# Fifty-one products of zeros placed among the early work of TensorE in an attention and MLP kernel

## The chip, the cores and the metric

The kernel runs on one core of one Trainium2 chip, as one launch. Time is device microseconds of that core. Each kernel was timed several times; the median is compared. One further execution of each was recorded by the hardware profiler, and its rows are those shown here. PE is TensorE, DVE is VectorE, ACT is ScalarE, POOL is GpSimd and SP is SyncE, which issues the DMAs.

## The reference

```python
# q, k, v: 4 batches x 8 heads x 1152 x 64
q_pool = q.reshape(B, H, S // 2, 2, D).mean(axis=3)          # 576 pooled queries per head
scores = q_pool @ k.transpose(0, 1, 3, 2) / np.sqrt(D)
scores = scores - np.max(scores, axis=-1, keepdims=True)
attn = np.exp(scores)
attn = attn / (np.sum(attn, axis=-1, keepdims=True) + 1e-09)
x = (attn @ v).transpose(0, 2, 1, 3).reshape(2304, 512)
h = x @ w_in                                                 # 512 x 2048
out = np.maximum(0.01 * h, h) @ w_out                        # 2048 x 512
```

## The kernel before

Attention goes over 32 heads (hd 0 to 31). For a head, K, Q and V are loaded (load_k, load_q, load_v); POOL adds the pairs of queries (q_sum, line 459); PE transposes K (k_tr, line 409, five transposes) and Q (q_tr, line 467, three) against an identity; ACT and DVE split the results into a high and a low part (k_hi, k_lo, q_hi, q_lo; lines 296, 425, 476 to 482). PE then forms score tiles of 128 queries by 384 keys (qk, line 515), fourteen steps in a head, and DVE reduces each to its maximum (vmax, line 518). The maxima are negated, transposed by PE (m_tr, line 529), copied (m_cp, line 533) and brought by a DMA (m_dma, line 536) into a row of the low part of Q. The second score product, transposed (qkt, lines 548 and 549, four products of 288 columns a tile), can then be exponentiated by ACT as it is (exp, line 553). POOL sums (esum, line 558), and PE multiplies by V (pv, line 566) and forms the row sums (r_mm, line 577). Weights are loaded and split meanwhile, and the MLP (l1, line 709; l2 and l2s, lines 790 to 824) follows block by block, partly among the attention.

The order on each engine is not written by hand. Every piece of work is a step with a priority (lower goes first), a cost on its engine in estimated us, dependencies, and the buffers that it takes. A scheduler (class Scheduler) simulates the engines with these costs while the program is built: it looks for the earliest time at which any pending step could start, and among the steps that can start by then takes the one with the lowest priority. A table of shifts (SHIFT) is added to the priorities by name and head. What the scheduler picks is emitted at once, so its order is the order of instructions on each engine. `deps` have to end first, `order` steps only have to have started, and `takes` names a buffer and the steps after which it is free again.

PSUM has eight banks; bank 5 is the tag "o", which pv takes for each head from its first half on, and the tag "xb" is the buffer in SBUF for a block of x, taken by x_load after the heads of the first batch. Banks 4 and 7, and for a time 6, are the tag "t" for transposes and score tiles. Ahead of the scheduler's steps the program makes the identity on POOL and clears five tiles on DVE (lines 1042 to 1046).

Of the kernel before, what the change touches and what calls it, by code (L numbers as in the profile page):

```python
# [19 lines left out]
RT = 0.5  # L20
AHEAD = 14
MT = 5
START = 200
MAXES = 4
PVP = 2.5
# [86 lines left out]
MLP = ("x_load", "x_hi", "x_lo", "ws_load", "l1", "post", "l2", "o_evac", "o_out")  # L112


def shift(name, n, *more):

    ends = PHASES["weights" if name in WEIGHTS else "mlp" if name in MLP else "attention"]
    part = {"w_f32": 0, "post": 1}.get(name)
    by = SHIFT.get(name if part is None else name + str(more[part]), ())
    phase = sum(n >= x for x in ends)  # L120
    return by[phase] if phase < len(by) else 0
# [132 lines left out]
def tile_pooled_attention_moe(  # L254
# [15 lines left out]
    nc = tc.nc  # L270
# [19 lines left out]
    ENG = {"ACT": nc.scalar, "DVE": nc.vector, "POOL": nc.gpsimd}  # L290

    def f32(t):
        return t.bitcast(F32)
# [43 lines left out]
    def new(tag, slot, dtype=None):  # L337
        own, i = slot[0]
        if own == "bank":
            return banks[:, i, :] if len(slot) == 1 else banks[:, i:i + len(slot), :]  # L340
        shape, dt = (shapes[tag], F32R) if tag in shapes else spec[tag][1:3]
        dt, shape = dtype or dt, list(shape)
        if own == tag:
            return sb.tile(shape, dt, tag=f"{own}{i}", name=own)
        n = 1
        for x in shape[1:]:
            n *= x
        t = sb.tile(FIXED[own] if own in FIXED else spec[own][1], dt, tag=f"{own}{i}", name=own)
        if len(t.shape) > 2:
            old = "abc"[:len(t.shape) - 1]  # L350
            t = t.rearrange(f"p {' '.join(old)} -> p ({' '.join(old)})")
        t = t[:shape[0], :n]
        names = "abcd"[:len(shape) - 1]
        return t.rearrange(f"p ({' '.join(names)}) -> p {' '.join(names)}", **dict(zip(names, shape[1:])))
# [130 lines left out]
        )  # L485

    qz = {}

    def q_side(hd, e, i):
        qz[hd] = 128 * i[0][1]  # L490
        nc.scalar.copy(out=qzs[:, qz[hd] + 64:qz[hd] + 128], in_=f32(qh[hd])[:, SP - 64:])
# [354 lines left out]
    def trs(*rows):  # L846
        return {"PE": sum(0.01 + 0.00077 * r for r in rows)}

    def act(n, psum=False):
        return (0.16 if psum else 0.19) + n / 1200.0  # L850

    def dve(n, rate=1, psum=False):
        return (0.15 if psum else 0.13) + n / 960.0 / rate
# [7 lines left out]
    def step(fn, *a, prio, eng, lat=0.0, deps=(), order=(), takes=(), lock=False):  # L861
        prio += shift(fn.__name__, *a)
        sch.add((fn.__name__, *a), partial(fn, *a), prio, eng, lat, [d for d in deps if d], [d for d in order if d], takes, lock)

    def sp(n, nbytes, run=512):
        return dict(eng={"SP": 0.5 * n}, lat=nbytes / 300e3 * max(1.0, 512 / run))

    for hd in range(NHD):
        p0 = 5.0 * hd
        pr = p0 - AHEAD - (0 if hd else START)  # L870
        prev = hd - 1 if hd else None

        def after(*key):
            return [(key[0], hd - 1, *key[1:])] if hd else []
# [4 lines left out]
        for g in range(2):  # L879
            hold = [(f, hd, x) for f in ("k_hi", "k_lo") for x in ((2,) if g else (0, 1))]  # L880
            step(k_tr, hd, g, prio=pr + 0.1 * g, eng=trs(*[128] * (1 if g else KT // 2)),
                 deps=[("load_k", hd)] + ([("k_tr", hd, 0)] if g else after("k_tr", 1)),
                 takes=[("t", hold, TR)] + ([] if g else [("ka", [last, ("k_dup", hd)])]))
            for x in (2,) if g else (0, 1):
                n = 128 if g else 512
# [6 lines left out]
        if 0 < hd < len(qls):  # L892
# [3 lines left out]
             takes=[("t", hold, TR), ("qh", [last]), ("ql", [last])])  # L896
        for x in range(2):
            for y in range(2):
# [3 lines left out]
             takes=[("qz", [("qk", hd, NQ - 1, 1)])])  # L902
        pm = p0 - MAXES - (0 if hd else START)
        ready = [("q_hi", hd, x, y) for x in range(2) for y in range(2)]
        todo = [(i, 0) for i in range(NQ)] + [(NQ - 1, 1)] + [(i, c) for c in (1, 2) for i in range(NQ - 1)]
        for n, (i, c) in enumerate(todo):
# [4 lines left out]
                 takes=[("t", [("vmax", hd, i, c)])] + ([] if n else [("st", [("m_tr", hd)])]))  # L911
            step(vmax, hd, i, c, prio=pm - 1 + 0.02 * n, eng={"DVE": dve(w, psum=True)}, deps=[("qk", hd, i, c)])
        step(m_side, hd, prio=pm - 2, eng={"ACT": act(2)}, deps=[("vmax", hd, NQ - 1, x) for x in range(2)])
        step(vneg, hd, prio=pm - 2, eng={"DVE": 0.17}, deps=[("m_side", hd)] + [("vmax", hd, *x) for x in todo])
        step(m_tr, hd, prio=pm - MT, eng=trs(128), deps=[("vneg", hd)], takes=[("t", [("m_cp", hd)])])
        step(m_cp, hd, prio=pm - 2, eng={"ACT": act(128, True)}, deps=[("m_tr", hd)], takes=[("ms", [("m_dma", hd)])])
        step(m_dma, hd, prio=pm - 2, **sp(1, 0.01e6), deps=[("m_cp", hd)], order=[("q_lo", hd, x) for x in range(2)])
        ready += [("k_lo", hd, x) for x in range(3)] + [("k_dup", hd), ("m_dma", hd)] + [("q_lo", hd, x) for x in range(2)]
        done = ("pv", hd, NBU - 1)
        ns = KT - 1 - direct(hd)  # L920
        for t in range(KT):
# [4 lines left out]
                 takes=[("e", [("pv", hd, b), ("esum", hd, max(t, 1)) if t <= ns else ("r_mm", hd)])])  # L926
            if 0 < t <= ns:
                step(esum, hd, t, prio=p0 - 4 + 0.5 * t, eng=pool(2 * HW, "esum" if hd < 14 else "late"), lock=True, deps=[("exp", hd, t), ("exp", hd, 0) if t == 1 else ("esum", hd, t - 1)],
                     takes=[("sm", [("r_mm", hd)])] if t == 1 else [])
        for b, (t0, t1) in enumerate(BURSTS):  # L930
            step(pv, hd, b, prio=p0 + 0.5 * t1 + PVP, eng=mm4(*[HW] * (t1 - t0)),
                 deps=[("exp", hd, t) for t in range(t0, t1)] + [("load_v", hd), ("pv", hd, b - 1) if b else ("pv", hd - 1, NBU - 1) if hd else None],
                 takes=[] if b else [("o", [("norm", hd)])])
        step(r_mm, hd, prio=p0 + 4.5 + RT, eng=mm4(*[HW] * ((2 + direct(hd)) // 2)), deps=[("esum", hd, ns)] + [("exp", hd, t) for t in range(ns + 1, KT)],
             takes=[("t", [("r_cp", hd)])])
# [13 lines left out]
    for n, i in enumerate(seq):  # L949
        o = i // NF  # L950
# [11 lines left out]
    for p in range(FH):  # L962
# [5 lines left out]
        for n in range(4):  # L968
            deps = [("w_sum", p, n % 2)] + ([("w_sum", p, 1)] + [("l2", FAST - 1, 0, 1, x) for x in (p,)] if n == 0 else [])
            takes = [("w2" if p == 0 and n == 1 else "w1", last)] if n and not (p == 0 and n == 2) else []  # L970
# [3 lines left out]
    for i in range(NBLK):  # L974
# [5 lines left out]
        order = [x * FH + p for p in range(FH) for x in (1, 0)] if fast else list(range(NF))  # L980
        for at, f in enumerate(order):
# [4 lines left out]
                 order=[("ws_load", i if at else i - 1, was) if at or i else None], takes=[("ws", [("l1", i, f, 2)], 0 if i else 1)])  # L986
            for part in range(3):
                dep = [("l1", i, f, part - 1) if part else prev, ("w_lo", 2 * NF - 1) if i == 1 and f == 0 else None]
                dep += [("ws_load", i, f), ("x_hi", i)] if part == 0 else [("x_lo", i)] if part == 1 else []
                takes, begun = [], []  # L990
                if part == 0 and at % 2 == 0:
                    if fast:
                        n = (i - FAST) * FH + fp - DEEP
                        begun = [("l2s", FAST + n // FH, n % FH, 0 if n % FH == FH - 1 else None)] if n >= 0 else []
                        takes = [("ml", [("g_act", i, fp)])]
                    else:
                        takes = [("ml", [("post", i, fp, 0)]), ("gg", [("l2", i, hf, 1, f + 1)], 0 if i else 1)]
# [11 lines left out]
        for p in range(FH if fast else 0):  # L1009
            banks_of = [[("o_mix", i, n) for n in x] for x in ((1,), (3,), (5, 7), (6,))]  # L1010
            for b in range(4) if p == FH - 1 else (None,):
                last = ("l2s", i, p, b - 1) if b else ("l2s", i, p - 1, None) if p else ("l2s", i - 1, FH - 1, 3) if i > FAST else ("l2", i - 1, 1, 1, NF - 1)
                n = 21 if b is None else 3 if b == 3 else 6
                step(l2s, i, p, b, prio=pr + p + LAG, eng=mm(*[256] * n), deps=[last, ("g_lo", i, p)] + [("w_rest", p, x) for x in range(4)],
                     takes=[("ml", x) for x in banks_of] if p == 0 else [])
        if fast:
            need = (0, 0, 1, 1, 2, 2, 3, 2)
            order_of = ((), (0,), (0, 1), (2,), (2,), (4,), (3, 4), (6,))
            for n in range(8):
                eng = {"DVE": dve(256, psum=True)} if n else {"ACT": act(256, True), "DVE": dve(256, psum=True)}  # L1020
                step(o_mix, i, n, prio=-50, eng=eng, deps=[("l2s", i, FH - 1, need[n])] + [("o_mix", i, x) for x in order_of[n]],
                     takes=[] if n else [("raw", [("o_mix_out", i, j)], 1) for j in range(2)])
# [3 lines left out]
        for hf in range(2):  # L1026
            for j in range(2):
                fs = range(hf * FH, hf * FH + FH)
                last = ("l2", i, hf, 0, fs[-1]) if j else ("l2", i, 0, 1, FH - 1) if hf else ("l2", i - 1, 1, 1, NF - 1) if i else None
                for f in fs:  # L1030
                    step(l2, i, hf, j, f, prio=pr + 15, eng=mm(512, 512, 512),
                         deps=[("l2", i, hf, j, f - 1)] if f != fs[0] else [last, ("w_lo", NF + fs[-1])] + [("post", i, x, 2) for x in range(hf * FP, hf * FP + FP)],
                         takes=[("ml", [("o_evac", i, hf, j)])] if f == fs[0] else [])
                step(o_evac, i, hf, j, prio=-50, eng={"DVE": dve(512, psum=True)} if hf else {"ACT": act(512, True), "DVE": dve(512, psum=True) + 0.3},
                     deps=[("l2", i, hf, j, fs[-1])] + ([("o_evac", i, 0, j)] if hf else []), takes=[] if hf else [("raw", [("o_out", i, j)], 1)])
# [42 lines left out]
```

## Time and profile before

| | us |
|---|---|
| median of 3 runs | 911.78 |
| lowest and highest | 909.09, 915.53 |
| the profiled execution | 910.16 |
| its span, first to last instruction | 908.4 |
| PE busy | 872.6 |
| DVE busy | 538.0 |
| ACT busy | 459.4 |
| POOL busy | 453.9 |

The profiled execution's time is compared with the medians, its span with the rows of the trace; 1.8 us lie around the span. Times in rows are us from the span's start.

### The profile page before, as it was taken

To read this page: it belongs to the slowest core of one execution; us is meant where nothing else is said; L and a number is where in the kernel's file an instruction comes from. 1 tells how busy PE (TensorE), PEld (TensorE's weight loads), DVE (VectorE), ACT (ScalarE), POOL (GpSimd) and SP (SyncE) were. 2 spreads that over 40 slices of the span, in tenths; PEclk is the share of its full clock that TensorE was granted. 3 is DMA by queue.
4 is the path that set the end of the run, shared out by engine and by line. 5 is a ranking of instruction groups with operands and counts; after the bars stand their busy time and mean duration, and the time that the engine had idled before them with its cause. 6 is when DMAs were issued, how large, how long until landed. Compare 5 with 4: busy or idle time off the path is not lost.

```text
span 908.4 us, 17330 instructions
## 1 busy us (share of the span) xinstructions
PE 872.6 (96%) x6408; PEld 731.9 (81%) x6408; DVE 538.0 (59%) x1140; ACT 459.4 (51%) x905; POOL 453.9 (50%) x352
## 2 busy tenths in 40 slices
PE   5898899999999999999999999999999999999997
PEld 3676666678877778887887888787898999999997
DVE  6788878777665655555455554601179863645343
ACT  3676786865656575545566555444143422323231
POOL 2457677686778676766676766766321010110000
PEclk9999999999999999999999999999999999999999
DMA  5588785865745854445367434434664767776660
GB/s 157 143 229 258 200 252 165 239 184 160 251 112 170 238 171 134 121 128 153 85 148 183 117 112 110 134 97 130 222 196 178 236 226 221 230 220 216 201 229 30
DMA packets 113269, 158.74 MB, mean 175 GB/s; under 512 B 21632, under 2 KB 80160, under 8 KB 113184
## 3 DMA queue, kind: packets, MB, share of 16 engines
q1 hardware_dynamic: 113184, 157.64, 59.2%
q8 instruction: 50, 0.82, 0.4%
q14 instruction: 35, 0.29, 0.1%
HBM read 130.02 MB, written 17.90 MB: 163 GB/s over the span
## 4 chain that ended last, share of the span: by engine, by line
PE 76%; DMA 12%; DVE 4%; ACT 3%; SPq 2%; issue 1%; POOL 0%; DVEq 0%; ACTq 0%; POOLq 0%
PE banks L709 21%; PE banks L566 11%; PE banks L790 11%; PE banks L515 7%; PE banks L548 7%; PE banks L549 6%; PE banks L822 3%; PE banks L824 3%; PE banks L823 3%; DMA rt<-rs 2%; DMA raw<-in_moe_w_out_dram 2%; DMA raw<-in_moe_w_in_dram 2%; PE banks L409 2%; PE banks L577 2%; DMA qn<-in_q_dram 1%
## 5 line engine op out<-in xcount | busy, mean ns | idle before, releaser
L553 ACT ACTIVATE e<-banks 128x576 f32<-128x576 f32 x288 | 185.4, 650 | 158.4 <-PE banks L549 156.1
L558 POOL TENSOR_TENSOR sm<-sm,e 128x576 f32<-128x576 f32 x168 | 242.8, 1446 | 44.0 <-ACT e L553 37.3
L518 DVE TENSOR_REDUCE stat<-banks 128x1 f32<-128x384 f32 (+1 forms) x448 | 218.9, 535 | 69.5 <-PE banks L515 64.5
L548 PE MATMUL banks<-qh,ka 128*128 128x288 f32 x576 | 171.2, 313 | 5.5 <-ACT e L553 5.3
L549 PE MATMUL banks<-ql,kb 128*128 128x288 f32 x576 | 161.5, 295 | 0.1
L709 PE MATMUL banks<-xb,ws 128*128 128x256 f32 x1152 | 159.6, 282 | 0.2 <-DVE xb L296 0.2
L566 PE MATMUL banks<-e,vv 128*64 128x288 f32 x1152 | 153.9, 412 | 0.0
L709 PEld LDWEIGHTS banks<-xb,ws 128*128 128x128 f32 x1152 | 150.2, 188 | 2.6 <-issue 1.4
L548 PEld LDWEIGHTS banks<-qh,ka 128*128 128x128 f32 x576 | 108.9, 189 | 30.7 <-ACT e L553 10.8
L566 PEld LDWEIGHTS banks<-e,vv 128*64 128x64 f32 x1152 | 76.9, 136 | 56.6 <-issue 9.6
L515 PE MATMUL banks<-ka,qh 128*128 128x384 f32 x384 | 110.1, 358 | 11.0 <-DVE stat L518 5.2
L549 PEld LDWEIGHTS banks<-ql,kb 128*128 128x128 f32 x576 | 109.0, 189 | 2.1 <-DMA ql<-ms 0.4
L425 DVE TENSOR_TENSOR ka<-banks,ka 64x512 fp32r<-64x512 f32 (+1 forms) x96 | 53.2, 554 | 67.7 <-ACT ka L296 66.0
L515 PEld LDWEIGHTS banks<-ka,qh 128*128 128x128 f32 x384 | 67.3, 191 | 24.4 <-DVE stat L518 11.6
L558 POOL TENSOR_TENSOR sm<-e 128x576 f32<-128x576 f32 x32 | 45.7, 1428 | 66.1 <-ACT e L553 66.1
L709 PE MATMUL banks<-ka,ws 128*128 128x256 f32 x576 | 72.1, 281 | 0.2 <-DMA ws<-wd 0.2
L709 PEld LDWEIGHTS banks<-ka,ws 128*128 128x128 f32 x576 | 70.0, 189 | 0.6 <-DMA ws<-wd 0.4
L790 PE MATMUL banks<-wo,gg 128*128 128x256 f32 x320 | 60.7, 282 | 0.0
L476 ACT ACTIVATE qh<-banks 64x288 fp32r<-64x288 f32 x127 | 51.4, 405 | 6.0 <-PE banks L467 3.5
L296 ACT CAST ka<-banks 64x512 fp32r<-64x512 f32 (+1 forms) x95 | 44.8, 472 | 10.6 <-PE banks L409 8.8
L459 POOL TENSOR_TENSOR qs<-qn 96x384 f32<-96x384 f32 x32 | 32.2, 1006 | 34.8 <-PE banks L467 26.3
L722 POOL TENSOR_TENSOR gg<-g,gg 128x512 fp32r<-128x512 f32 x29 | 37.3, 1285 | 23.6 <-ACT gg L296 14.8
(185 smaller groups left out, 1232.7 us busy)
## 6 DMA issues: line engine op xcount, KB each, us to landing
ws<-wd SPq DMA_DIRECT2D x144, 512.0 KB, 4.3
qn<-in_q_dram SPq DMA_DIRECT2D x32, 288.0 KB, 4.8
kn<-in_k_dram SPq DMA_DIRECT2D x32, 288.0 KB, 3.3
vv<-in_v_dram SPq DMA_DIRECT2D x32, 288.0 KB, 5.0
kb<-ka SPq DMA_DIRECT2D x64, 128.0 KB, 4.2
raw<-in_moe_w_in_dram SPq DMA_DIRECT2D x16, 512.0 KB, 5.3
wd<-ws SPq DMA_DIRECT2D x16, 512.0 KB, 2.8
raw<-in_moe_w_out_dram SPq DMA_DIRECT2D x16, 512.0 KB, 4.9
```

The costliest lines, as they stand in the source:

```text
L296: ENG[e].copy(out=out, in_=in_) if e == "ACT" else ENG[e].tensor_copy(out=out, in_=in_)
L425: nc.vector.tensor_tensor(out=d[64 - o:128 - o], in0=src, in1=f32(d[o:o + 64]), op=ALU.subtract)
L476: nc.scalar.activation(out=dst, in_=src, func=AF.Copy, scale=QSCALE)
L515: nc.tensor.matmul(p, lhsT=lhsT, rhs=ka[hd][:, k0:k0 + w], start=(j == 0), stop=(j == 128 // n - 1))
L518: nc.vector.tensor_reduce(out=mx[hd][:, i, c:c + 1], in_=mps.pop((hd, i, c)), axis=AX.X, op=ALU.max)
L548: nc.tensor.matmul(p[:, hf, :HW], lhsT=ka[hd][:, ks], rhs=qh[hd][:, c], start=True, stop=False)
L549: nc.tensor.matmul(p[:, hf, :HW], lhsT=kb[hd][:, ks], rhs=ql[hd][:, c], start=False, stop=True)
L553: nc.scalar.activation(out=ex[hd, t], in_=sps.pop((hd, t))[:, :, :HW], func=AF.Exp)
L558: ENG[e].tensor_tensor(out=sm[hd], in0=ex[hd, 0] if t == 1 else sm[hd], in1=ex[hd, t], op=ALU.add)
L566: nc.tensor.matmul(p[64 * hf:64 * hf + 64, :HW], lhsT=vv[hd][:, t, :], rhs=ex[hd, t][:, hf], start=(t == 0), stop=(t == KT - 1),)
L709: nc.tensor.matmul(p, lhsT=wst[i, f][:, a, c, :], rhs=xx[i][x][:, c, :], start=(n == 0), stop=(n == 3 * KC - 1))
L790: nc.tensor.matmul(o, lhsT=g[i, p][:, a], rhs=w[:, x], start=(p == 0 and n == 0 and half == 0), stop=(p == FH - 1 and n == 2), skip_group_ ...
```

## The change

Two new functions are emitted as steps. warm_zero takes the buffer "xb" and the bank "o", both until the last of the new products, and clears a 128x128 part of the buffer on DVE. warm is a product of this part (128 columns of weights) with its own first 64 columns, into bank "o"; nothing reads the result. There are 51 of them, in a chain. Their priority is 1e6, so the scheduler takes one only where no other step can start by that time; the cost given is 0.2 us of PE. The first eleven depend on the clearing alone; the twelfth may start once k_tr of head 0's second group (its fifth K transpose) has started. The function shift gets a default for its second argument, as warm_zero has no number. Nothing is removed.

```diff
+WARM = (11, 40)
...
-def shift(name, n, *more):
+def shift(name, n=0, *more):
...
     qz = {}
+    idle = []
+
+    def warm_zero(e, i, i2):
+        idle.append(new("xb", i)[:, 0, 0, :128])
+        idle.append(new("o", i2)[:, :64])
+        ENG[e].memset(f32(idle[0]), 0.0)
+
+    def warm(n, e):
+
+        nc.tensor.matmul(idle[1], lhsT=idle[0], rhs=idle[0][:, :64], start=True, stop=True)
...
+    done = [("warm", sum(WARM) - 1)]
+    step(warm_zero, prio=-1e6, eng={"DVE": 0.2}, takes=[("xb", done), ("o", done)])
+    for n in range(sum(WARM)):
+        step(warm, n, prio=1e6, eng={"PE": 0.2}, deps=[("warm_zero",)] + ([("warm", n - 1)] if n else []), order=[("k_tr", 0, 1)] if n == WARM[0] else [])
```

## Rows read from the trace of the kernel before

**Rows 1.** The page's first part: busy time, share of the span and instructions.

```profile
PE 872.6 (96%) x6408; PEld 731.9 (81%) x6408; DVE 538.0 (59%) x1140; ACT 459.4 (51%) x905; POOL 453.9 (50%) x352
```

**Rows 2.** Busy time by stage; columns: PE, PEld, DVE, ACT, POOL, PEclk, DMA share, GB/s.

```profile
0.00:27.80 27.80, 15.74 (x53) 11.29 (x54) 18.14 (x38) 11.79 (x29) 7.76 (x17) 1.00 0.62 162
...
40.00:50.00 10.00, 8.19 (x56) 5.30 (x53) 9.44 (x19) 5.84 (x15) 1.99 (x2) 1.00 0.74 206
50.00:100.00 50.00, 45.89 (x338) 32.77 (x336) 42.40 (x81) 35.14 (x73) 31.98 (x25) 1.00 0.88 246
100.00:200.00 100.00, 92.98 (x693) 68.00 (x691) 78.67 (x163) 75.27 (x157) 76.08 (x59) 1.00 0.73 211
200.00:632.00 432.00, 426.38 (x3042) 342.50 (x3043) 229.00 (x488) 240.99 (x489) 298.43 (x228) 1.00 0.52 145
632.00:908.40 276.40, 271.32 (x2155) 262.89 (x2153) 152.12 (x336) 82.98 (x133) 29.51 (x18) 1.00 0.62 200
```

**Rows 3.** Timeline of PE, 0 to 27.8 us: start, duration, instruction, idle before.

```profile
5.02 1.09 PE L409 MATMUL banks<-ident,kn 128*128 128x128 f32 x4 [5.02 <-DMA kn<-in_k_dram]
...
9.40 0.98 PE L515 MATMUL banks<-ka,qh 128*128 128x384 f32 x2 [2.60 <-DVE ka L425]
10.71 1.15 PE L515 MATMUL banks<-ka,qh 128*128 128x384 f32 x2 [0.33 <-DVE stat L518]
...
16.87 0.71 PE L467 MATMUL banks<-ident,qs 96*128 96x96 f32 x3
...
20.29 0.42 PE L529 MATMUL banks<-ident,neg 128*64 128x128 f32 x1 [1.64 <-DVE ql L482]
21.22 1.41 PE L409 MATMUL banks<-ident,kn 128*128 128x128 f32 x5 [0.51 <-ACT ms L533]
...
25.02 1.33 PE L409 MATMUL banks<-ident,kn 128*128 128x128 f32 x5 [1.69 <-DVE ka L425]
...
26.63 0.44 PE L548 MATMUL banks<-qh,ka 128*128 128x288 f32 x1
26.87 0.44 PE L549 MATMUL banks<-ql,kb 128*128 128x288 f32 x1
```

**Rows 4.** Timeline of PE after 27.8 us.

```profile
28.60 0.29 PE L548 MATMUL banks<-qh,ka 128*128 128x288 f32 x1
28.73 0.29 PE L549 MATMUL banks<-ql,kb 128*128 128x288 f32 x1
29.02 0.45 PE L515 MATMUL banks<-ka,qh 128*128 128x384 f32 x1
...
37.59 0.44 PE L467 MATMUL banks<-ident,qs 96*128 96x96 f32 x3
37.96 0.66 PE L409 MATMUL banks<-ident,kn 128*128 128x128 f32 x4
```

**Rows 5.** Timeline of DVE, 0 to 18 us.

```profile
0.99 0.33 DVE L1044 MEMSET qzs<- 128x320 f32 x1
...
6.76 0.69 DVE L296 CAST ka<-banks 64x512 fp32r<-64x512 f32 x1 [3.47 <-ACT ka L296]
...
10.10 1.02 DVE L518 TENSOR_REDUCE stat<-banks 128x1 f32<-128x384 f32 x2
11.44 1.02 DVE L518 TENSOR_REDUCE stat<-banks 128x1 f32<-128x384 f32 x2 [0.32 <-PE banks L515]
...
13.00 4.66 DVE L518 TENSOR_REDUCE stat<-banks 128x1 f32<-128x288 f32 x10
```

**Rows 6.** Groups of PE's instructions, 0 to 27.8 us: busy us, mean ns.

```profile
L409 PE MATMUL banks<-ident,kn 128*128 128x128 f32 x16 | 4.4, 429 | 7.2 <-DMA kn<-in_k_dram 5.0 <-DVE ka L425 1.7 <-ACT ms L533 0.5
L467 PE MATMUL banks<-ident,qs 96*128 96x96 f32 x9 | 2.1, 374 | 0.0
```

**Rows 7.** Timeline of the SP queue at head 0's maxima.

```profile
22.94 0.84 SPq L536 DMA_DIRECT2D ql<-ms  x1
```

**Rows 8.** Waits of PE, 27.8 to 200 us: total, times, longest.

```profile
PE banks L529 <- DVE neg L525: 1.9, 3, 1.3
```

## Prediction

> **What bounds the kernel now.** I read the page's busy shares first: PE is busy for 872.6 us of the 908.4 us span, no other engine for more than 59% [rows 1]. So a change pays only where it shortens PE's fixed work or fills or removes PE's idle time, and I went to the table by stage to see where the idle 35.8 us lie [rows 2]: 12.06 us stand before 27.8 us (27.80 less 15.74 busy), 1.8 us from 40 to 50, 4.1 from 50 to 100, 7.0 from 100 to 200, 5.6 from 200 to 632, and 5.1 behind that, most of it the tail after the last product. The stretch that the change touches by its own instructions is the first one alone.
>
> Next I read PE's timeline there. The table's clock column prints 1.00 for the first stretch too, but the durations say otherwise: two QKT products of 288 columns start 0.24 us apart at 26.63 and 26.87 [rows 3], which is 1.2 GHz, and 0.13 us apart at 28.60 and 28.73 [rows 4], which is the 2.4 GHz level. Four K transposes take 1.09 us at 5.02 and 0.66 us at 37.96, three Q transposes 0.71 and 0.44 us. So PE runs at the lower level until about 27.8 us and at the upper one afterwards. What it did before that one rise: it had worked without a gap since 25.02. What it did before without a rise: it worked from 5.02 to 6.80, sat idle 2.60 us, worked in short pieces to about 18.6, and then had idle gaps of 1.64, 0.51 and 1.69 us [rows 3].
>
> The lower clock costs little of this, since other engines set much of the pace. In the longest piece, from 13.00, ten reductions on DVE take 4.66 us, 0.466 us each [rows 5]; a 384-column score product streams for 0.32 us at the lower level (0.24 times 384/288), so DVE ends last there at either level.
>
> **The change part by part.**
>
> *The clearing.* One DVE memset of 128x128 is put behind the five memsets ahead of the plan. A larger one of 128x320 takes 0.33 us, so I count 0.1 to 0.33. DVE then waits 3.47 us for ACT until 6.76 [rows 5], so its memsets end at about 3.3, and this wait hides the new one. The first filler can start at about 3.5.
>
> *Eleven fillers before the first transposes.* No row has a product of 64 columns under weights of 128. Low bound: its columns alone, 0.24 times 64/288 = 0.053 us. High bound: the whole step of a transpose of 128 columns, (1.09 - 0.43)/3 = 0.22 us. The nearest row is the Q transpose, which loads 128 columns of weights for each short product: (0.71 - 0.374)/2 = 0.17 us a step [rows 3, 6]. I take 0.17, since here too the weights are long against the product. Eleven end at 3.5 + 1.9 = 5.4, between 4.1 and 5.9 at the bounds. The first transposes start at 5.02 and everything on PE is queued behind, so this costs about 0.3 us (0 to 0.9). The Trainium skill, TensorE: Matmul & The Clock Gate, section "LDWEIGHTS (loading the stationary operand)", prices a weight load at its columns over 1.2, which is 107 ns for 128; by that the eleven would end at 4.7 and cost nothing.
>
> *Forty fillers behind the first K transposes.* Their priority is the last, and the planner prices each at 0.2 us of PE, so it puts one wherever its own PE is free first. In its costs the reduction of one score tile takes 0.15 + 384/960 = 0.55 us and the product 0.18, so about two fillers fit between two products; the wait that shows as 2.60 us at 9.40 [rows 3] takes about a dozen. So I expect the forty to be used up around the end of head 0's fourteen score steps, about 17 us. On PE they stand in order between products that wait for banks anyway. At the lower clock two fillers and a product need 2 x 0.17 + 0.32 = 0.66 us against DVE's 0.466, so while the clock is still low each such pair costs up to 0.2 us, at most 1.7 us over the last ten; at the upper level all halves to 0.33 us and DVE hides it.
>
> *What the clock may give back.* With the fillers PE has hardly a gap from 3.5 to about 17, as it had none ahead of the one rise in the trace. I assume a rise shortly before 9.4 and that it holds through the three short gaps that follow. On the path to the first QKT product then stand: the first score product, 0.7 us from 9.40 to its reduction at 10.10 against 0.45 for a lone one at 29.02 [rows 3 to 5]: 0.23; the third one, after which DVE waits 0.32 us [rows 5]: 0.24; head 1's Q transposes, 0.71 to 0.44: 0.27; head 2's K transposes at 21.22, 1.41 for five, so 1.13 for the four that are converted first, against 0.66: 0.47; head 3's five at 25.02, 1.33 against about 0.8: 0.53. Sum 1.74 us. To the lone transpose of the maxima at 20.29 (0.42, so some 0.1) and to the first QKT products I choose to give nothing, as ACT has conversions of K and Q beside both; the latter's worth stands in the bound. Against that stand two limits: the DMA of head 0's maxima is issued only at 22.94 [rows 7], is needed by the product ahead of 26.63, and moves with the parts ahead of 21 us only (0.74 of the 1.74); no row shows it to be late, so I keep the whole sum. And nothing can give more than half of PE's 15.74 us there, 7.9 us, 0.9% of the span.
>
> I take 1.7, less 0.3 for the first eleven: 1.4 us. Bounds: no gain with 2.6 us of cost (0.9 + 1.7), or 3.1 us of gain (the first transposes, 0.43, and eight QKT products at 0.13 instead of 0.24, 0.9, on top). The gain keeps to the end, as later stages issue their loads from steps of PE and ACT and move left as a whole.
>
> *The plan behind it.* Fifty-two new steps with costs move the planner's times for PE by parts of 0.2 us, and every later choice of the list follows from such times and from priorities with small shifts. So the order on all engines can differ far behind the fillers, at no cost in work. This has no row; its bounds are the idle time that an order can remove or add. After 200 us PE is idle for 5.6 us in 432, so little can be gained there; between 40 and 200 it is 12.9 us. I take zero for it, and 7 us either way as its reach.
>
> **The sum.** The profiled execution took 910.16 us, span 908.4 and 1.8 around it; it gives 908.8. Its median of three is 911.78, 1.6 above, and the three lie 6.4 us apart. Against the median: 911.8 - 1.4, so **910.4 us**. That is 0.15%, well under the 1% that a measurement of this kernel can tell from no change.
>
> **The rivals.**
>
> *The clock doesn't rise earlier*, or falls back in the gaps after 17 us: the change doesn't do what it says. For it: with work in pieces from 9.4 to 18.6 there was no rise, and a filler streams 0.053 us of its 0.17; also the transposes of 5.02 to 6.80 may add nothing. Against it: the one rise came after 2.8 us without a gap, of which the first third was transposes. It would give the costs alone, 0 to 2.6 us: 911.8 to 914.4, say 913. The Trainium skill says this of transposes: in the same page, section "Part 4: PE-mode transpose", the full clock does not engage for them, as they don't count as busy in the same way. The rise at 27.8 behind five transposes and seven products doesn't contradict or confirm it.
>
> *The new order makes PE wait more* (the slower side). Place: heads 1 to 7, 40 to 200 us, where a maximum's transpose or a score product comes up on PE before DVE has released it. Price: the longest wait of this kind is 1.3 us now [rows 8]. One more eats most of the gain; seven, one in each head, give 9.1 - 1.4 = 7.7 us more, **919.5**; from nine on it would be over 1% (11.7 - 1.4 = 10.3). For it: in this stage DVE and DMA are nearly as full as PE, 42.40 of 50 us and 0.88 from 50 to 100 [rows 2], so an order that is off by half a microsecond finds no slack. Against it: the planner makes the new order with the same costs and rules as the old one.
>
> *The new order makes PE wait less.* By the same rows: half of the 12.9 us between 40 and 200 goes, with the clock's 1.4: **904**. It would take an order that is better by chance.
>
> **How the numbers follow.** The forecast has 0.45 (own range 907.5 to 913), the clock that doesn't rise 0.15, the order that costs 0.18, the one that gains 0.15, anything else 0.07. About 0.4 of each order case lies beyond 1%, and the rest is split: faster by over 1% 0.10, slower by over 1% 0.10, within it 0.80. The range reaches over both order cases to about their middle, 903 to 919.
>
> **What would show it.** In the profile after: 51 products of 64 columns, eleven of them between 3.5 and about 5.4 (their step settles 0.053 against 0.17), the rest before 17 us; score products of head 0 with 0.34 to 0.45 us instead of 0.67; K transposes at 21 and 25 us with 0.66 for four; the first QKT product near 24.5 instead of about 26. Transposes that still take 1.1 us would show that the clock is low; a first transpose after 5.2, that the eleven are too many. The prediction is wrong if the table by stage shows other idle sums after 40 us than now by more than 3 us: then the order decided, and not the clock.

## The result, and the profile after

The changed kernel took 920.61 us (median of 4, 919.75 to 924.4) beside 911.34 for the kernel before: ratio 1.0104, interval 1.0058 to 1.0151. Timed again beside others on another chip it gave 1.0071 (1.0049 to 1.0093, 12 runs). So it is slower by 0.7 to 1.0%. The forecast was 910.4 with a range up to 919. Three executions that lie more than 1.5% above the fastest of their kernel (3064.25 us of the kernel called the order alone below, 1062.19 and 924.54 us of the kernel before) are left out of all ratios.

The profiled execution spans 919.4 us, 11.0 more than before. The page's first part after, against [rows 1]:

```profile
PE 886.7 (96%) x6459; PEld 746.5 (81%) x6459; DVE 538.2 (59%) x1137; ACT 461.4 (50%) x909; POOL 454.1 (49%) x352
```

PE has 51 more products and is busy for 14.1 us more. Some of that filled idle time, so I looked at the first stretch: the timeline of PE after, against [rows 3]. Line 498 is one of the new products (a filler), 410 K's transposes, 526 the score product, 559 and 560 the second score product (QKT).

```profile
3.58 2.56 PE L498 MATMUL banks<-xb 128*128 128x64 f32 x11 [3.58 <-DVE xb L494]
5.95 1.11 PE L410 MATMUL banks<-ident,kn 128*128 128x128 f32 x4
...
7.41 2.96 PE L498 MATMUL banks<-xb 128*128 128x64 f32 x13
10.35 0.66 PE L526 MATMUL banks<-ka,qh 128*128 128x384 f32 x1
...
18.24 0.67 PE L526 MATMUL banks<-ka,qh 128*128 128x384 f32 x1
18.70 0.47 PE L498 MATMUL banks<-xb 128*128 128x64 f32 x2
18.99 0.67 PE L526 MATMUL banks<-ka,qh 128*128 128x384 f32 x1
...
21.14 1.11 PE L410 MATMUL banks<-ident,kn 128*128 128x128 f32 x4
...
28.66 1.33 PE L410 MATMUL banks<-ident,kn 128*128 128x128 f32 x5 [1.69 <-DVE ka L426]
...
33.36 0.30 PE L559 MATMUL banks<-qh,ka 128*128 128x288 f32 x1
33.49 0.29 PE L560 MATMUL banks<-ql,kb 128*128 128x288 f32 x1
```

Three things are to be seen. A filler takes 0.21 us ((2.56 - 0.40)/10, and (2.96 - 0.40)/12), so the eleven end at about 5.9 and the first transposes start at 5.95 instead of 5.02. The score products with two fillers between them come 0.75 us apart (18.24, 18.99), where before DVE set 0.466. And the clock stays low: four transposes still take 1.11 us at 21, and the QKT products come 0.13 us apart only from 33.36 on; before it was from about 27.8. The timeline of DVE after shows who waits in the score products: each reduction of 0.56 us now stands alone, behind a wait for PE, where ten followed each other without one [rows 5].

```profile
18.20 0.56 DVE L529 TENSOR_REDUCE stat<-banks 128x1 f32<-128x384 f32 x1 [0.19 <-PE banks L526]
18.95 0.56 DVE L529 TENSOR_REDUCE stat<-banks 128x1 f32<-128x384 f32 x1 [0.19 <-PE banks L526]
```

So the bound of this stretch passed from DVE to PE. The first exponential, which was at 27.54 in the trace of before, is late by 3.63 us; the timeline of ACT after:

```profile
31.17 1.42 ACT L564 ACTIVATE e<-banks 128x576 f32<-128x576 f32 x2
```

The table of busy time by stage gives the rest, against [rows 2]. Columns: PE, PEld, DVE, ACT, POOL, PEclk, DMA share, GB/s.

```profile
0.00:27.80 27.80, 21.50 (x92) 20.00 (x92) 16.74 (x34) 8.76 (x22) 6.84 (x16) 1.00 0.51 137
...
40.00:50.00 10.00, 8.41 (x62) 5.08 (x61) 8.04 (x17) 6.92 (x16) 2.66 (x3) 1.00 0.65 170
50.00:100.00 50.00, 45.28 (x311) 32.75 (x312) 40.65 (x80) 32.27 (x65) 32.03 (x25) 0.97 0.80 223
100.00:200.00 100.00, 93.12 (x689) 66.94 (x685) 78.47 (x159) 76.26 (x159) 71.48 (x57) 0.98 0.74 210
200.00:632.00 432.00, 425.17 (x3035) 341.08 (x3032) 233.60 (x497) 242.17 (x495) 294.67 (x225) 1.00 0.53 145
632.00:919.40 287.40, 281.91 (x2219) 271.07 (x2217) 152.43 (x337) 87.83 (x142) 39.65 (x24) 1.00 0.61 198
```

PE's idle time before 27.8 us fell from 12.06 to 6.30, yet the work behind it starts later: the idle time was a wait for others, and filling it brought nothing. PE's idle time from 200 to 632 grew from 5.6 to 6.8. The clock column shows short falls that the profile of before doesn't have; the same table cut at them:

```profile
33.30:91.30 58.00, 51.69 (x366) 36.91 (x367) 45.20 (x92) 37.88 (x78) 34.08 (x27) 1.00 0.76 208
91.30:94.70 3.40, 3.40 (x17) 1.36 (x13) 3.40 (x4) 0.72 (x2) 3.32 (x3) 0.50 0.69 262
...
142.50:145.90 3.40, 3.40 (x16) 1.84 (x16) 3.33 (x8) 1.21 (x3) 3.24 (x3) 0.50 0.13 26
...
340.50:343.90 3.40, 3.40 (x16) 1.42 (x12) 0.51 (x2) 0.00 (x0) 1.40 (x1) 0.50 0.20 43
```

In three stretches of 3.4 us PE runs at 1.2 GHz, each worth up to 1.7 us. That tempted me to call them a part of the loss. The other traces speak against it: the second recorded execution of the changed kernel has no such fall between 33.6 us and its last 3 us and still took 918.42 us, and kernels below that keep the order of before have them as well (one fall, at 47.2 us, in the kernel with thirteen fillers, 909.50 us; four with all 51, 922.42 us). The recorded execution of before happened to have none, and its 910.16 us lie below every median of that kernel, 911.34 to 914.68 us; so a distance from its rows can hold some us that are not the change's.

The instruction orders of the two kernels settle the rest of the picture. PE's order without the fillers is the same for the first 1113 products (to 186 us in the trace of before), and so is that of the other engines up to about the same steps of the plan, but for one operation on Q's low part (q_lo), which DVE does two reductions earlier at the start. Then head 9's products by V come ahead of head 11's third score step, and from there on all five engines differ: 194 of PE's 1575 steps stand elsewhere, for instance.

### The profile page after: what moved, and what is told of

Same layout as the page of the kernel before. It is cut to its first block, busy times and chain, and to the rows that moved or that the text cites. A ratio compares the mean times of both kernels' runs of the same rounds, so it can differ in the third digit from the quotient of the medians.

```text
span 919.4 us, 17428 instructions
## 1 busy us (share of the span) xinstructions
PE 886.7 (96%) x6459; PEld 746.5 (81%) x6459; DVE 538.2 (59%) x1137; ACT 461.4 (50%) x909; POOL 454.1 (49%) x352
## 4 chain that ended last, share of the span: by engine, by line
PE 77%; DMA 10%; DVE 5%; ACT 3%; SPq 2%; issue 2%; POOL 0%; DVEq 0%; ACTq 0%
PE banks L720 20%; PE banks L577 12%; PE banks L801 11%; PE banks L526 8%; PE banks L559 7%; PE banks L560 6%; PE banks L833 3%; PE banks L835 3%; PE banks L834 3%; DMA rt<-rs 2%; DMA raw<-in_moe_w_in_dram 2%; DMA raw<-in_moe_w_out_dram 2%; PE banks L588 2%; PE banks L410 2%; DMA xb<-xd 1%
## 5 line engine op out<-in xcount | busy, mean ns | idle before, releaser
L577 PE MATMUL banks<-e,vv 128*64 128x288 f32 x1152 | 158.3, 421 | 0.0
L559 PEld LDWEIGHTS banks<-qh,ka 128*128 128x128 f32 x576 | 109.3, 190 | 32.2 <-issue 12.3
L526 PE MATMUL banks<-ka,qh 128*128 128x384 f32 x384 | 112.5, 360 | 10.3 <-DVE stat L529 7.2
L801 PEld LDWEIGHTS banks<-wo,gg 128*128 128x128 f32 x320 | 47.8, 188 | 0.4 <-DVE gg L787 0.4
```

Source lines behind the costliest of these rows:

```text
L526: nc.tensor.matmul(p, lhsT=lhsT, rhs=ka[hd][:, k0:k0 + w], start=(j == 0), stop=(j == 128 // n - 1))
L559: nc.tensor.matmul(p[:, hf, :HW], lhsT=ka[hd][:, ks], rhs=qh[hd][:, c], start=True, stop=False)
L577: nc.tensor.matmul(p[64 * hf:64 * hf + 64, :HW], lhsT=vv[hd][:, t, :], rhs=ex[hd, t][:, hf], start=(t == 0), stop=(t == KT - 1),)
L801: nc.tensor.matmul(o, lhsT=g[i, p][:, a], rhs=w[:, x], start=(p == 0 and n == 0 and half == 0), stop=(p == FH - 1 and n == 2), skip_group_ ...
```

## The experiments

Two theories. *The fillers*: their own time on PE, at the low clock, delays the start, and that stays to the end. *The order*: the fillers' costs shift the plan, and the new order from 186 us on (head 9's products by V) makes PE wait more. All times are ratios to the kernel before on the same chip in the same round of runs, whose median was 914.35, 914.68 and 913.37 us in the three rounds.

**The order alone, and the fillers alone.** The first leaves the plan of the changed kernel and emits nothing for its 52 steps:

```diff
     def warm_zero(e, i, i2):
-        idle.append(new("xb", i)[:, 0, 0, :128])
-        idle.append(new("o", i2)[:, :64])
-        ENG[e].memset(f32(idle[0]), 0.0)
+        pass
...
-        nc.tensor.matmul(idle[1], lhsT=idle[0], rhs=idle[0][:, :64], start=True, stop=True)
+        pass
```

The second is the kernel before, its plan untouched, with fillers emitted ahead of named steps; a table FILL says how many:

```diff
+FILL = {('k_tr', 0, 0): 11, ('qk', 0, 0, 0): 13, ('qk', 0, 1, 0): 1, ('qk', 0, 2, 0): 4, ...}
...
+        for _ in range(FILL.get(s.key, 0)):
+            self.filler()
         s.run(e, *got)
...
         zero_q(0, "DVE")
+        z = new("xb", (("xb", 0),))[:, 0].rearrange("p c n -> p (c n)")
+        nc.vector.memset(f32(z)[:, :128], 0.0)
+        sch.filler = lambda: nc.tensor.matmul(banks[:128, 5, :64], lhsT=z[:, :128], rhs=z[:, :64], start=True, stop=True)
         sch.run()
```

> The order of the changed kernel, planned with the 51 fillers and their costs, but neither they nor their clearing are emitted. The theory of the fillers (their own time on PE at the low clock, 3.6 us by the first exponential, and what follows from it) expects the time of before, 911 us within 2, and the first exponential at 27.5 us. The theory of the order (the plan differs from head 9 on) expects the larger part of the 9 us to stay, 916 to 920. If both have a part, by the trace of after (7.8 us late at head 9, 11.0 at the end) the order has about 3 us: 914.

> The order of before, kept as it was, with the 51 fillers emitted at the places that they have in the changed kernel. The theory of the fillers expects 917 to 920 us, the first exponential 3.6 us late (31.2), and short falls of the clock behind idle times of PE over 1.6 us. The theory of the order expects 912 to 914: the lateness of the start is partly made up behind it.

Measured: the order alone 1.0040 (1.0013 to 1.0067), the fillers alone 1.0049 (1.0028 to 1.0071). Neither theory is the whole: both effects are there, of about equal size, and together they make 0.9%. In the profile of the fillers alone the first exponential is at 31.28, 3.75 us late, as in the changed kernel.

**The two parts of the fillers.** FILL cut to its first entry, and FILL without it.

> The order of before with the first eleven fillers alone. At 0.213 us each they end at 5.95 and delay the first transposes by 0.93 us: the theory of the fillers expects 912 to 913 us and the clock's rise at about 28.7 us or one step of it away. A theory that the fillers raise the clock early when they are not spread among score products expects a rise before 10 us and a gain of 1 to 2 us.

> The order of before with the other forty fillers alone, at their places. The theory of the fillers expects the score products of head 0 to come 0.74 us apart instead of 0.47, the first exponential 2.7 us late, and 914 to 917 us. The theory of the order expects no more than 913.

Measured: the eleven 1.0006 (0.9984 to 1.0029), the forty 1.0052 (1.0033 to 1.0070). The eleven delay the first transposes to 5.94 and head 1's Q transposes to 17.81, by 0.9 us both. The first exponential, at 28.20, is only 0.66 us late, because the clock was up from 16.7 to 20.1 us in this trace: three Q transposes take 0.44 us instead of 0.71, as the timeline of PE of the eleven shows.

```profile
17.81 0.44 PE L470 MATMUL banks<-ident,qs 96*128 96x96 f32 x3
18.18 0.77 PE L412 MATMUL banks<-ident,kn 128*128 128x128 f32 x5
```

That is too little for the timing to show. So the expectation of the clock, a rise at 28.7 us or before 10, held for neither theory: it rose at 16.7, fell at 20.1 and rose again at 30.3. The forty delay the first exponential by 2.71 us and, as far as the intervals tell, bring all of the measured loss.

**The changed kernel and its order once more.**

> The changed kernel once more, beside the others on one chip. If the order alone (+0.4%) and the fillers alone (+0.5%) are its parts, +0.9%, between 0.7 and 1.1. The theory of the order alone or of the fillers alone would have it at no more than +0.5%.

> The order of the changed kernel without fillers, again, for its profile and a second interval. First exponential at 27.5 us as before; no more than 1 us late until head 9, since all engines have the order of before until there but for one operation of DVE; and late by 2 to 5 us between heads 9 and 31. +0.2 to +0.6%. The theory of the fillers expects the profile of before, within the falls of the clock.

Measured: the changed kernel 1.0071 (1.0049 to 1.0093), the order alone 1.0028 (0.9997 to 1.0059). This second interval for the order just holds 1; the first didn't. The sum of the parts, 0.77% with the fillers' 0.49, agrees with this, and within its interval with the first result. In the trace of the order alone the first exponential is at 26.49, 1.05 us early: 0.30 us of it by the moved operation of DVE (the maxima of head 0 are negated at 17.47 instead of 17.77), the rest with the clock, which in this trace, with no filler at all, was up from 14.6 to 21.5 us. Head 11's first score product, where the orders part, comes 1.16 us late, head 31's 3.82, so 2.7 us come in the stretch where the order differs.

One trace could show this by chance, so here is the same stretch, from head 11's first score product to head 31's, in all traces without a fall of the clock in it: 389.2 to 392.0 us in the seven that have the order of before, 392.70 and 394.19 us in the two that have the new one. PE's idle time from 200 to 632 us is 3.6 to 5.7 us in the seven and 6.3 and 7.0 us in the two. The waits of PE there, 195 to 632 us (total, times, longest), in the kernel before:

```profile
PE banks L548 <- ACT e L553: 2.8, 4, 1.0
PE banks L515 <- DVE stat L518: 2.4, 2, 1.3
```

and in the order alone, where the score product is line 524:

```profile
PE banks L524 <- DVE stat L527: 4.0, 6, 1.1
PE banks L557 <- ACT e L562: 1.5, 4, 0.7
PE banks L524 <- DVE ka L426: 1.2, 2, 0.6
```

and in the changed kernel:

```profile
PE banks L526 <- DVE stat L529: 4.9, 5, 2.1
PE banks L559 <- ACT e L564: 1.1, 3, 0.5
```

So the score products wait for DVE's reductions 1.6 to 2.5 us more, in six and five waits instead of two, and the second score products (lines 548, 557 and 559) wait 1.3 and 1.7 us less for the exponential. In the other trace of the changed kernel the wait for the reductions is 3.9 us; in the seven with the order of before it is 1.3 to 3.3. This is the mechanism that the prediction priced for heads 1 to 7, later and smaller. Which reduction comes late, and by which step of the plan, was not followed.

**Narrow weights.** The fillers at their places with 32 columns of weights (lhsT=z[:, :32], output on 32 partitions).

> The order of before with all 51 fillers at their places, but with 32 columns of weights instead of 128. If the load of the weights is what makes a filler take 0.213 us at the low clock, it takes 0.053 us now (32 columns at the same price a column), the score products come 0.47 us apart again, the first exponential is less than 0.5 us late, and the time is that of before within 0.2%. If a filler's price is a fixed one or its product's, the pitch stays near 0.7 us and the time at +0.4 to +0.5%.

Measured: 1.0028 (1.0005 to 1.0052), first exponential at 28.89, 1.35 us late. The timeline of PE of this kernel, where line 1052 is the filler and 518 the score product:

```profile
3.51 0.79 PE L1052 MATMUL banks<-xb 128*32 128x64 f32 x11 [3.51 <-DVE xb L1051]
5.07 1.08 PE L412 MATMUL banks<-ident,kn 128*128 128x128 f32 x4 [0.77 <-DMA kn<-in_k_dram]
...
15.86 0.67 PE L518 MATMUL banks<-ka,qh 128*128 128x384 f32 x1
16.33 0.31 PE L1052 MATMUL banks<-xb 128*32 128x64 f32 x2
16.45 0.67 PE L518 MATMUL banks<-ka,qh 128*128 128x384 f32 x1
```

Among themselves the fillers now take 0.053 us each ((0.79 - 0.26)/10), as expected: the load of 128 columns made the 0.21. But the score products come 0.59 us apart, not 0.47. So half of my expectation fell. Nothing else stands between them on PE, and the clock was low as before, so it is the two short products that break the sequence. A sum fits the rows: a score product's columns take 0.32 us at this clock, and behind them one load is hidden; behind a short product the next load is not, 0.05 us for the second filler and 0.21 us for the score product, 0.59 in all. With full weights the same sum gives 0.32 + 2 x 0.213 = 0.75 us for two fillers and 0.53 us for one, as the rows of the changed kernel above and of the 27 below have it. The load of the score product itself was not varied.

**Where a filler stands.** FILL cut to the thirteen ahead of the first score product, and to the 27 behind it.

> The order of before with thirteen of the forty fillers alone, those ahead of the first score product. Thirteen at 0.213 us take 2.8 us against a wait of 2.6: first exponential less than 0.2 us late, time that of before within 0.2%. A theory that every filler costs its 0.213 us wherever it stands expects +0.3%.

> The order of before with the other 27 of the forty alone, ahead of the second score product and later ones. If the loads of weights behind short products set the pace, the score products come 0.75 us apart, the first exponential is about 2.7 us late as with all forty, and the time is +0.3 to +0.5%. By the theory of an equal price in every place +0.6%.

Measured: the thirteen 0.9993 (0.9974 to 1.0013), the 27 1.0037 (1.0013 to 1.0061). The timelines of PE, first of the thirteen:

```profile
6.55 2.96 PE L1052 MATMUL banks<-xb 128*128 128x64 f32 x13
9.50 0.98 PE L518 MATMUL banks<-ka,qh 128*128 128x384 f32 x2
```

then of the 27:

```profile
14.49 0.67 PE L518 MATMUL banks<-ka,qh 128*128 128x384 f32 x1
14.95 0.26 PE L1052 MATMUL banks<-xb 128*128 128x64 f32 x1
15.02 0.67 PE L518 MATMUL banks<-ka,qh 128*128 128x384 f32 x1
15.49 0.47 PE L1052 MATMUL banks<-xb 128*128 128x64 f32 x2
15.77 0.67 PE L518 MATMUL banks<-ka,qh 128*128 128x384 f32 x1
```

Thirteen in a wait of 2.6 us are hidden, at 0.21 us each, and so is the clearing: the first exponential is 0.09 us late, but so are the first transposes (5.12 instead of 5.02, when their DMA landed). Behind a score product one filler makes the distance to the next 0.53 us and two make it 0.75. The first exponential of the 27 is 2.64 us late, though the first transposes came 0.15 us early (4.87). Counted from the transposes, the three groups cost 0.93 us, nothing and 2.79 us: 3.72, against 3.63 to 3.75 us for all 51 together.

**Wide products, and only in waits.** These keep the order of before and put the clearing first on DVE; the products have 512 columns, so that a load of weights is hidden behind each (they come 0.43 us apart at the lower clock, their columns alone). The first has eight ahead of the first transposes and five ahead of the first score product. The other two have seven more in the three waits of PE from 17 to 25 us, and one of them a product of 256 columns ahead of each later score product as well:

```diff
+FILL = {('k_tr', 0, 0): [512] * 8, ('qk', 0, 0, 0): [512] * 5, ('m_tr', 0): [512] * 3, ('k_tr', 2, 0): [512], ('k_tr', 3, 0): [512] * 3}
...
+        for n in FILL.get(s.key, ()):
+            self.filler(n)
...
         make_identity(nc, ident)
+        z = new("xb", (("xb", 0),))[:, 0].rearrange("p c n -> p (c n)")
+        nc.vector.memset(f32(z)[:, :512], 0.0)
         nc.vector.memset(stats[0], LOWEST)
```

> The order of before with thirteen wide products of zeros (512 columns, 0.43 us each at the low clock) instead: eight from about 1.5 us, with the clearing put first on DVE, and five ahead of the first score product; none among the score products. If gapless streaming raises the clock early, it rises before 10 us, transposes at 17 us take 0.66 us for four, and the time is 1 to 2 us under that of before, or, where the clock falls again in the gaps after 17 us, the same. If products of zeros don't raise it, it rises at about 28 us and the time is that of before or 0.5 us over.

> The order of before with 20 products of zeros of 512 columns, eight from 1.5 us, five ahead of the first score product, seven in the three waits of PE from 18 to 25 us, and one of 256 columns ahead of each later score product. If the clock rises early and stays up while PE has work, it is up from about 7 us to the end, the first exponential is 1 to 2.5 us early, and the time is -0.1 to -0.3%. If the clock is low among the score products, they come 0.53 us or more apart and the time is +0.1 to +0.2%.

> As the kernel before it, without the products among the score products: they stand only in waits of PE. If the clock falls in the score products (35% of the pace at the upper clock) and does not rise again before 25 us, as with the thirteen wide ones alone, the time is that of before or 0.2% under; if the seven later ones raise it again, the four K transposes at 20 us take 0.66 us and the first exponential is 1 to 2 us early.

Measured: wide and early 0.9983 (0.9955 to 1.0011), with the score products held too 0.9976 (0.9950 to 1.0003), in the waits alone 0.9965 (0.9943 to 0.9988). The last is the only kernel here whose interval lies below the kernel before, by 0.1 to 0.6%. In all three traces the clock rises early, at 6.8, 7.1 and 5.5 us, and falls again: the table by stage of the first, then that of the last, cut at the changes.

```profile
6.80:13.60 6.80, 4.52 (x17) 2.44 (x15) 6.54 (x14) 1.59 (x6) 2.82 (x6) 1.00 0.75 190
13.60:30.60 17.00, 13.17 (x48) 10.25 (x48) 11.68 (x24) 10.05 (x25) 5.13 (x6) 0.50 0.50 138
```

```profile
5.50:12.30 6.80, 4.24 (x21) 2.75 (x19) 5.47 (x11) 2.10 (x6) 2.42 (x7) 1.00 0.84 230
12.30:19.20 6.90, 6.90 (x21) 4.53 (x19) 5.38 (x14) 2.34 (x6) 2.05 (x3) 0.51 0.19 47
19.20:22.60 3.40, 2.21 (x13) 1.36 (x13) 2.17 (x5) 2.56 (x8) 0.04 (x1) 1.00 0.68 195
22.60:26.00 3.40, 2.98 (x12) 2.22 (x11) 2.45 (x5) 2.81 (x8) 1.58 (x2) 0.50 0.76 195
```

In the first it falls among the score products, and the later rise, at 30.6, is later than that of before: the first exponential is only 0.48 us early. With a product of 256 columns between them the clock stayed up to 20.7 us, the score products kept DVE's pace, and the exponential came 1.07 us early. In the last the transposes of 20.58 take 0.66 us for four, as at the upper clock, and the timeline of ACT shows the first exponential 1.10 us early:

```profile
26.44 1.18 ACT L556 ACTIVATE e<-banks 128x576 f32<-128x576 f32 x2
```

1.1 us are 0.12%, the edge of the interval; its recorded execution, at 916.25 us the slowest of its twelve, doesn't show where more could come from. So that much of the idea behind the prediction's gain was there, in a form that the change doesn't have.

## Why the prediction was wrong

The step that failed is the gain by the clock: "I assume a rise shortly before 9.4 and that it holds". With these fillers the clock rose at 33.3 us, later than before: PE worked on 24 fillers and eight transposes from 3.6 to 10.3 us with no rise, while with the wide products of zeros, from 1.5 us on, it rose at 5.5 to 7.1 us in all three traces. None of the five savings on the path came, so 1.74 us fell out of the sum. (The first of them is 0.25 by its own figures, 0.70 less 0.45, not 0.23.)

The price of a filler, 0.17 us, was 0.21, close to the upper bound, 0.22, that I had worked out from the transposes and not taken. For the eleven this made 0.93 us at the first transposes instead of 0.3. The Trainium skill's rule, from TensorE: Matmul & The Clock Gate, section "LDWEIGHTS (loading the stationary operand)", columns over 1.2, gives an estimate of 107 ns for 128 columns; the trace has twice that, and the narrow weights show that it is the load. All fillers of this form ran at the lower clock and with this element type, so which of the two makes the difference stays open.

The cost of the others among the score products was taken as nothing at the upper clock and at most 1.7 us at the lower one. It is 2.6 to 2.8 us. The distance that I had computed for two fillers and a score product, 0.66 us, came out as 0.75: the same sum with the right price, 2 x 0.213 + 0.32. And I counted the last ten steps alone, where fillers stand ahead of each of the thirteen later ones. The same page's section "Step-by-step: what each phase is for" says that the next weights load while a product runs. The trace agrees as long as the product is long: two score products at 9.40 take 0.98 us, one 0.67, so they come 0.31 us apart, their columns alone. Behind a product of 64 columns little of a load is hidden.

That the thirteen in the long wait are free was right, and so was the count of fillers ahead of the first score product and the stretch where they end (21.9, not 17, as PE was late).

"I take zero for it, and 7 us either way": the order costs 0.3 to 0.4%, about 3 us, in waits of score products for DVE. It was named as a rival with the right mechanism, in the wrong heads (the plan's order is the same up to 186 us), and held apart from the fillers' cost. This is the second fault, one of form: the range was made of cases that exclude each other, with the fillers' cost (up to 2.6 us) in one and the order's in another. They were independent, and both came: 3.6 and about 3 us, 0.7%, and with the first result's own uncertainty 1.0%. A case that holds both would have stood at 911.8 + 3.6 + 3, about 918.4. The sign given for the order, idle sums after 40 us that differ by more than 3 us, was too coarse to see it: they are 25.5 us after and 23.6 before.

That PE bounds the kernel, so that a shift of the start keeps to the end, was right: the timed losses of the kernels with all 51 fillers, the forty and the 27 in the order of before, 4.5, 4.8 and 3.4 us, are no smaller than the delays of their first exponentials, 3.75, 2.71 and 2.64 us.

## What to carry to other kernels

Before work is put into an engine's idle time, read what ends that time: a wait for one event of 2.6 us takes thirteen short products for nothing, while the 0.15 us left in each step of a pipeline is there only as long as the next step's load of weights stays hidden. Short products under full weights cost their load here, not their columns; where PE was to be kept streaming, few long products did it, at no cost in true waits. And where a planner makes the order, place such products after planning, as the kernels with FILL do: a change that does no work still moves the order of everything behind it.

## What was not expected of the hardware

The clock's rise in the first 35 us differs from trace to trace. With no filler at all it rose at 27.8 us in one and at 14.6 in the other, where it fell again at 21.5; with the first eleven it rose at 16.7. These are different kernels with one trace each, so whether the run or the kernel decides is open; the two traces of the changed kernel have it at 33.3 and 33.6. After a rise it fell, with the wide products early and in waits, in score products that DVE paces (at 13.6 and 12.3 us), behind waits of PE of 1.43 and 1.76 us up to 9.4 us and none over 0.50 from there on. Later falls stood behind waits of PE of 1.67, 1.95 and 2.07 us in the changed kernel's trace, and waits up to 1.34 us in the trace of before had none behind them; but in the second recorded execution of the changed kernel a wait of 2.56 us had none either, and the fall at 47.2 us in the trace of the thirteen came after no wait over 0.95 us since 25.1, so the length of a wait alone doesn't tell. The table's clock column prints 1.00 for the stretch ahead of the first recorded change; durations tell that it is low.
